# Sixteen unread TensorE products ahead of a planned attention and gate kernel

## The chip, the cores and the metric

The kernel runs on one core of a Trainium2 chip. The metric is the device time of one execution in microseconds (us). Five engines work side by side, each through its own instructions in order: TensorE (PE, with its weight loads shown apart as PEld), VectorE (DVE), ScalarE (ACT), GpSimd (POOL) and SyncE (SP, which here only issues DMAs). They wait for each other through semaphores.

## The reference: what is computed

Inputs are q, k, v of shape (4, 8, 768, 64), centroids (8, 16, 64), w_proj (512, 1536), filter_fft (768, 512) and w_out (512, 512), all float32. The output is (4, 768, 512). In the reference's terms, cut to what matters:

```
q_assign, k_assign = argmax over 16 centroids of the normed q, k
scores = q k^T / sqrt(64), -1e9 where q_assign and k_assign differ
attn = softmax(scores) @ v                      # per batch and head
x1, x2, x3 = split(attn as (4, 768, 512) @ w_proj)
x2_conv = irfft(rfft(x2) * rfft(filter_fft))    # along the 768 tokens
out = (x1 * x2_conv * x3) @ w_out
```

## The kernel before, in words

**Work.** Eight groups n of four heads (two groups for each batch) go through three steps. *Routing* turns q and k by TensorE transposes (the function `tr` in `routing`, line 592, issued at L594, for the first two groups; `tr2`, L583, later), copies them out of PSUM (helper `copy`, L265, on ACT or DVE), multiplies them with the normed centroids (`sim`, L503 for the first group, L614 later), copies that out, transposes it back (L513, L627) and lets DVE find the largest (L520 to L527, L635 to L652). The result becomes 16 more rows of the operands of the scores. *Attention* works on pairs of heads, with six steps sk of 128 keys: scores (function `sc`, issued at L73 or L75, into one PSUM bank each), exponentials on ACT (L697, L700) into a buffer p, the product with v (`pv`, L711, into the PSUM pair of banks 4 and 5), and a running sum of the p on DVE (`part` L728, `acc` L732) for the denominators. At the end of a pair ACT copies the result out (L735), the denominators go through TensorE (`den` L745) or DMAs, and DVE writes the normed result xT (L811). For the very last pair this goes without DMAs: `den` L745, `total` on ACT L751, `dT` L793, a reciprocal on DVE L796, `bc` L802, xT L811. *Hyena* takes each batch after its second group: the middle third of the projection (L845), folds on DVE (L859, L864), the spectrum (L466), its product with the filter (L875, L879), the first and last third of the projection in single products of 0.65 us (function `G`, line 904, issued at L75; its bank is emptied by a copy L913 or a multiplication L916 on DVE), the way back (function `I`, line 923, whose result DVE takes out at L941 or L951, with a copy at L939), the gate (L954) and w_out (line 964).

**Order.** None of this is issued in the order of the program text. `op` records every step with its possible engines, a guessed duration and a due time; `Plan.place` then plays the steps through in time, gives each to an engine and a PSUM bank, and among the steps that could start within 0.1 us takes the one with the earliest due time. The table NUDGE moves single due times and ONLY fixes engines, so order and banks can be set step by step. What is built is an order for each engine, which the chip then follows whatever the times are. `banks_for` gives banks by class: "head" may use banks 4 and 5 until the first `pv`, "fill" may not.

**Start.** POOL makes the identity (`constants`), the first loads of q, k and the centroids go out on SP and ACT, DVE makes the angles of the transform tables (L355 to L362) between the steps of the centroids (L319 to L330), and ACT takes their square root and the sines (L322, L365, L367), with a table load ahead of each kind. TensorE's first instructions are the six transposes of the first q (L594), then the transpose of the centroids (L333), then twelve transposes (L594), then the first eight instructions of `sim` (L503).

Of the kernel before, what the change touches and what calls it, by code (L numbers as in the profile page):

```python
# [35 lines left out]
LEAD = 2.99901  # L36
FIRST = 2
BUSY = 8.09741
# [5 lines left out]
HOLD = {"score": "score", "o": "o"}  # L44
AFTER = {"PE": .16}
OVERLAP = {"ACT": .09, "DVE": .08}
MODES = {"pv": 64, "bc": 64, "half": 64, "sim": 32, "den": 32, "score": 0, "proj": 0, "inv": 0}


def array(o, last):  # L50
# [27 lines left out]
class Plan:  # L78
# [6 lines left out]
    def op(self, eng, fn, due, r=(), w=(), alloc=None, free=(), lock=False, byts=0, after=(), kind=None, lat=0.0):  # L85
# [15 lines left out]
        for key in w:  # L101
            self.writers[key] = [o]
            self.reads[key] = []
        deps.discard(o)
        o.deps = deps
        o.left = len(deps)
        for d in deps:
            d.outs.append(o)
        for h in free:
            h.readers += 1  # L110
        self.ops.append(o)
        return o

    def place(self, free0, banks_for, switch=0.1, wait=0.1, rate=215e3, bonus=10.84378, margin=0.02195, shape=1.63806):
        free = dict(free0)
        bank_free = [0.0] * 8
        ready = {e: [] for e in free}
        pend = 0
        st = SimpleNamespace(pool=0.0, dve=0.0, bw={}, last=None, kind=None, score=0, o=0, tail=0,
                             held=dict(score=0, fill=0, o=0))  # L120
        st.scores, st.otiles = (sum(o.alloc is not None and o.alloc.cls == c for o in self.ops) for c in ("score", "o"))
        busy = dict.fromkeys(free, 0.0)

        def enqueue(o):
            o.ready = max([d.end - AFTER.get(d.on, 0.0) * (d in o.soft) + (0.06 if o.eng.keys().isdisjoint((d.on,)) or d.byts else 0.0)
                           for d in o.deps] or [0.0])
            if o.kind == "load":
                o.ready = max(o.ready, o.due - LEAD)
            for e in o.eng:
                ready[e].append(o)  # L130

        def take(o):
            if o.alloc is None:
                return
            o.alloc.ids = banks_for(o.alloc, bank_free, st, o)[0]
            for i in o.alloc.ids:
                bank_free[i] = 1e9
            st.score += o.alloc.cls == "score"
            st.o += o.alloc.cls == "o"
            st.held[HOLD.get(o.alloc.cls, "fill")] += o.alloc.n  # L140
            if o.alloc.cls != "o":
                st.tail |= st.o == st.otiles and any(i in (4, 5) for i in o.alloc.ids)

        def done(o, e, t, d, end):
            o.start, o.on = t, e
            o.end = end + AFTER.get(e, 0.0)
            if o.byts:
                s, b = max(o.end + 1.3, st.bw.get(e, 0.0)), o.byts / rate
                for f in [f for f in st.bw if f != e and st.bw[f] > s]:
                    b += min(o.byts / rate, st.bw[f] - s)  # L150
                    st.bw[f] += min(o.byts / rate, st.bw[f] - s)
                st.bw[e] = s + b
                o.end = st.bw[e] + 0.6 + o.lat
            if e == "POOL" and o.lock:
                st.pool = t + d
            if e == "DVE" and o.lock:
                st.dve = t + d
            for h in o.free:
                h.readers -= 1
                h.end = max(h.end, o.end)  # L160
                if not h.readers:
                    st.held[HOLD.get(h.cls, "fill")] -= h.n
                    for i in h.ids:
                        bank_free[i] = h.end + 0.06
            for x in o.eng:
                ready[x].remove(o)
            for x in o.outs:
                x.left -= 1
                if not x.left:
                    enqueue(x)  # L170

        for o in self.ops:
            if o.seq in ONLY:
                o.eng = {ONLY[o.seq]: o.eng[ONLY[o.seq]]}
        for o in self.ops:
            if not o.left:
                enqueue(o)
        while any(ready.values()):
            best = None
            for e, lst in ready.items():  # L180
                f = free[e]
                cand = []
                for o in lst:
                    t = max(f, o.ready)
                    m = margin if e == "PE" else 0.0
                    late = max(f, o.ready + m)
                    if o.alloc is not None:
                        ids = banks_for(o.alloc, bank_free, st, o)
                        if ids is None:
                            continue  # L190
                        t, late = max(t, ids[1]), max(late, ids[1] + m)
                    if o.lock and e in ("POOL", "DVE"):
                        t = late = max(t, st.dve if e == "POOL" else st.pool)
                    cand.append((late, o, t))
                if not cand:
                    continue
                t0 = min(c[0] for c in cand)
                c = min((c for c in cand if c[0] <= t0 + wait + 1e-9), key=lambda c: (
                    c[1].due - (bonus if e == "PE" and st.kind == "pv" == c[1].kind else 0.0)
                    + (shape if e == "PE" and array(c[1], st.last) != st.last else 0.0)  # L200
                    + (BUSY if e == "DVE" and len(c[1].eng) > 1 else 0.0)
                    + (c[0] - t0) * 20, c[1].seq))
                if best is None or (t0, c[0]) < best[0]:
                    best = ((t0, c[0]), e, c[1], c[2])
            if best is None:
                raise RuntimeError("stuck: " + repr([(e, [x.kind for x in l][:4]) for e, l in ready.items()]))
            _, e, o, t = best
            take(o)
            d = o.eng[e]
            if e == "PE":  # L210
                mode = array(o, st.last)
                if mode != st.last:
                    d += switch
                st.last, st.kind, o.whole = mode, o.kind, mode == 128
            done(o, e, t, d, t + d)
            busy[e] += d - OVERLAP.get(e, 0.0)
            free[e] = t + d - OVERLAP.get(e, 0.0)
        self.busy = busy
        self.span = max(o.end for o in self.ops)
        return sorted(self.ops, key=lambda o: (o.start, o.seq))  # L220
# [27 lines left out]
def build(T):  # L248

    P = Plan()  # L250
    op = P.op
# [31 lines left out]
    def qk(z, ch):  # L283
        return [("qkT", z, i) for i in (((0,), (1, 2)), ((0, 1), (2,)))[z % 2][ch]]

    def dma(e):
        return (T.nc.scalar if e == "ACT" else T.nc.sync).dma_start

    def alu(e):
        return T.nc.vector if e == "DVE" else T.nc.gpsimd  # L290

    EV384 = {"ACT": .465, "DVE": .55}
    EV512 = {"ACT": .585, "DVE": .68}


    qslot, loads = {}, []

    def load_qk(n, pr, j, due, after=()):
        s = qslot[n, pr, j] = len(loads) % NQK
        loads.append(1)  # L300

        return [op({"SP": .8, "ACT": .8} if n == 0 else ("SP", .8), lambda e, hp=hp: dma(e)(
            T.qkraw[s][:, :, hp], (T.q, T.k)[j][n // 2, 4 * (n % 2) + 2 * pr + hp].rearrange(
                "(p t) d -> p t d", t=NT)), due, w=[("qkraw", s, hp)], byts=196e3, kind="load", after=after, lat=.5)
            for hp in range(2)]

    def load_v(n, pr, due, after=()):
        op(("SP", .6), lambda e: T.nc.sync.dma_start(
# [73 lines left out]
    def tables(got):  # L382

        FW = [("fw", m, cs) for m in range(3) for cs in range(2)]
        fv = lambda: T.filt.rearrange("(w p m e) d -> w e p m d", w=2, p=64, m=3, e=2)
        for w_ in range(2):
            for e_ in range(2):
                op(("SP", .7), lambda e, w_=w_, e_=e_: T.nc.sync.dma_start(
                    T.f[w_][64 * e_:64 * e_ + 64], fv()[w_, e_]), 16.0, w=[("f", w_, e_)], byts=393e3, kind="load", after=got)
        for j in range(6):  # L390
            h = Bank("head")
            due = 20.0 + 2 * j

            def tr(e, j=j, h=h):
                tp = ap(h).bitcast(BF16)
                for m in range(2):
                    cols = (0, 192, 0, 192, 128, 320)[j]
# [165 lines left out]
    def routing(n):  # L563
# [41 lines left out]
        if n == 0:  # L605
            return got + first_masks(1)
        b0 = end - 24.04235
        b0 -= EARLY * (n == 1)
        h = Bank(cls, 2)

        def sim(e, h=h):
            for ch in range(2):
# [4 lines left out]
           kind="sim")  # L617
# [610 lines left out]
```

## Time and profile before

| what | value |
| --- | --- |
| median of three executions | 383.94 us (383.84 to 384.43) |
| the profiled execution | 384.85 us |
| its span, first to last instruction | 383.1 us |
| busy: PE, DVE, ACT, POOL | 364.8, 347.5, 261.6, 108.6 us |
| first PE instruction | 4.63 us |
| PE waits, longest two | 4.7 us for the first q, 2.8 us for the centroids |
| DMA | 47.19 MB, mean 123 GB/s |

All views come from one execution. The page gives busy times and 40 slices of the span. The chain of waits follows the work that ended last back from the end, each piece with its start, its length and what it was. The timeline of one engine gives start, length, line, operation, tiles and count of its instructions, merged where equal ones follow each other, and in brackets the idle time just before and what ended it. Since instructions of one engine overlap at their edges, the time from one start to the next is what one of them costs.

### The profile page before, as it was taken

The numbers are of one execution on the slowest core, as the hardware profiler recorded it, in microseconds if no ns is written. First come the engines' busy times: TensorE is split into PE (matmuls) and PEld (weight loads), VectorE is DVE, ScalarE is ACT, GpSimd is POOL, SyncE is SP. The second block draws the span as 40 slices with busy tenths as digits, with TensorE's granted clock in tenths as the row PEclk, the third lists the DMA queues.
The fourth block names the chain that finished last, engine by engine and source line by source line (L and its number), as shares of the span: only waits on it lengthen the run. The fifth ranks groups of instructions, "written<-read, shape, count | busy, mean of one in ns | idle before, by whom it ended". The sixth has DMA issues, their size and how long they took to land.

```text
span 383.1 us, 8652 instructions
## 1 busy us (share of the span) xinstructions
PE 364.8 (95%) x3323; PEld 208.3 (54%) x3328; DVE 347.5 (91%) x519; ACT 261.6 (68%) x488; POOL 108.6 (28%) x147
## 2 busy tenths in 40 slices
PE   2999998999999999999999999999999999999895
PEld 1564454445445565655555565656554565567682
DVE  8878997999899999989998999989999999899992
ACT  5996979787883978858856569688863747623332
POOL 8432101100022544123432453133320442103600
PEclk9999999999999999999999999999999999999999
DMA  9719965762578587747796876855555642110214
GB/s 221 160 47 220 164 154 135 158 146 63 128 165 157 104 130 151 126 90 122 160 144 147 165 191 134 173 72 89 103 75 132 134 105 37 46 43 2 94 74 164
DMA packets 93861, 47.19 MB, mean 123 GB/s; under 512 B 82088, under 2 KB 87676, under 8 KB 93820
## 3 DMA queue, kind: packets, MB, share of 16 engines
q1 hardware_dynamic: 88620, 37.03, 39.9%
q0 software_dynamic: 2704, 8.98, 17.6%
q10 hardware_dynamic: 2496, 0.62, 0.7%
q8 instruction: 26, 0.43, 0.5%
q14 instruction: 15, 0.12, 0.1%
HBM read 31.59 MB, written 7.40 MB: 102 GB/s over the span
## 4 chain that ended last, share of the span: by engine, by line
PE 55%; DVE 22%; DMA 9%; ACT 7%; issue 5%; SPq 1%; POOL 0%; POOLq 0%; DVEq 0%; ACTq 0%
PE bank L75 22%; PE pair L711 18%; DVE acc L732 5%; DMA rb<-dr 5%; PE bank L845 4%; ACT p L700 3%; DVE tm L875 2%; PE bank L583 2%; PE bank L594 2%; PE bank L614 1%; DVE acc L728 1%; DMA dr<-dn 1%; ACT p L697 1%; DVE xT L811 1%; PE bank L503 1%
## 5 line engine op out<-in xcount | busy, mean ns | idle before, releaser
L711 PE MATMUL pair<-p,vraw 128*64 128x385 f32 x768 | 142.5, 490 | 0.9 <-ACT osb L735 0.6
L700 ACT ACTIVATE p<-bank 128x512 f32<-128x512 f32 x192 | 108.9, 604 | 31.9 <-PE bank L75 26.5
L732 DVE TENSOR_TENSOR acc<-p,acc 128x1536 f32<-128x1536 f32 x64 | 113.0, 1765 | 4.9 <-ACT p L697 2.3
L711 PEld LDWEIGHTS pair<-p,vraw 128*64 128x64 f32 x768 | 53.7, 136 | 49.6 <-issue 42.5
L75 PE MATMUL bank<-aug,aug 80*64 80x512 bf16 (+3 forms) x688 | 75.2, 327 | 2.2 <-DVE den L753 0.5
L697 ACT ACTIVATE p<-bank 128x512 f32<-128x512 f32 x96 | 57.2, 606 | 11.6 <-PE bank L75 10.8
L75 PEld LDWEIGHTS <-aug 128*64 128x64 bf16 (+1 forms) x688 | 40.5, 109 | 38.9 <-issue 28.6
L765 POOL DMA_DIRECT2D acc<-acc x30 | 23.8, 793 | 91.1 <-DMA acc<-acc 42.6
L75 PE MATMUL bank<-xT,wpj 128*64 128x384 bf16 x488 | 44.7, 326 | 0.0
L267 POOL CAST aug<-qkP 64x768 bf16<-64x768 f32 x22 | 20.3, 927 | 71.7 <-DVE acc L732 34.1
L265 ACT COPY qkP<-bank 128x512 f32<-128x512 f32 (+1 forms) x52 | 26.7, 543 | 15.9 <-PE bank L75 8.6
L75 PEld LDWEIGHTS <-wpj 128*64 128x64 bf16 x488 | 29.6, 110 | 13.9 <-issue 3.8
L75 PEld LDWEIGHTS <-y 128*64 128x64 bf16 x512 | 25.5, 110 | 14.4 <-issue 4.4
L728 POOL TENSOR_TENSOR acc<-p,p 128x512 f32<-128x512 f32 x13 | 16.5, 1275 | 53.2 <-ACT p L700 25.7
L875 DVE TENSOR_TENSOR tm<-bank,hm 128x512 f32<-128x512 f32 x44 | 27.9, 681 | 1.0 <-POOL y L879 0.2
L728 DVE TENSOR_TENSOR acc<-p,p 128x512 f32<-128x512 f32 x35 | 24.6, 730 | 2.7 <-ACT p L697 1.7
L265 ACT CAST aug<-qkP 64x768 bf16<-64x768 f32 x29 | 24.0, 831 | 1.6 <-PE bank L75 1.1
L879 POOL TENSOR_TENSOR y<-tm 128x512 bf16<-128x512 f32 x17 | 21.7, 1289 | 10.5 <-DVE tm L875 6.3
L845 PE MATMUL bank<-wpj,xT 128*64 128x512 bf16 x192 | 22.7, 380 | 0.9 <-DVE xT L811 0.9
L75 PE MATMUL bank<-wout,y 128*64 128x512 bf16 x192 | 22.9, 379 | 0.0
L735 ACT COPY osb<-pair 128x770 f32<-128x770 f32 x16 | 12.9, 808 | 9.6 <-PE pair L711 9.5
L811 DVE SCALAR_TENSOR_TENSOR xT<-osb,rb 128x768 bf16<-128x768 f32 x15 | 15.2, 1012 | 3.9 <-DMA rb<-dr 3.9
(161 smaller groups left out, 440.7 us busy)
## 6 DMA issues: line engine op xcount, KB each, us to landing
qkraw<-in_k_dram SPq DMA_DIRECT2D x32, 192.0 KB, 4.6
vraw<-in_v_dram SPq DMA_DIRECT2D x16, 384.0 KB, 4.3
rb<-dr SPq DMA_DIRECT2D x30, 192.0 KB, 3.3
out_dram<-ob SPq DMA_DIRECT2D x11, 512.0 KB, 2.8
qkraw<-in_q_dram SPq DMA_DIRECT2D x29, 192.0 KB, 3.9
acc<-acc POOLq DMA_DIRECT2D x10, 384.0 KB, 4.9
acc<-acc POOLq DMA_DIRECT2D x10, 192.0 KB, 4.1
y<-in_moe_filter_fft_dram SPq DMA_DIRECT2D x4, 384.0 KB, 8.9
```

The lines of the kernel that those rows point to most:

```text
L75: T.nc.tensor.matmul(out[64 * i:64 * i + 64], lhsT[:, 64 * i:64 * i + 64], rhs, start=start, stop=stop)
L265: T.nc.scalar.copy(out, in_)
L267: (T.nc.vector if e == "DVE" else T.nc.gpsimd).tensor_copy(out, in_)
L697: T.nc.scalar.activation(o, ap(h).rearrange("p (a b) -> p a b", a=2), Act.Exp, scale=0.125)
L700: T.nc.scalar.activation(flat(s)[:, lo:lo + 512], ap(h), Act.Exp, scale=0.125)
L711: T.nc.tensor.matmul(o[64 * hp:64 * hp + 64, ch, :385], T.vraw[vs][:, hp, sk * D:(sk + 1) * D], T.p[slots[sk]][:, hp, 384 * ch:384 * ch + ...
L728: alu(e).tensor_tensor(o, x, y, op=Alu.add)
L732: T.nc.vector.tensor_tensor(T.acc[os], T.p[slots[sk]][:, :, :S], T.acc[os], op=Alu.add)
L765: op(("POOL", .8), lambda e, rows=rows: T.nc.gpsimd.dma_start(flat_()[:rows], flat_()[rows:2 * rows], accum_op=Alu.add), te, r=[], w=AK, b ...
L845: T.nc.tensor.matmul(ap(h)[64 * i:64 * i + 64], T.xT[xs][:, kt, c:c + 64], T.wpj[:, kt, DM:2 * DM], start=kt == 0, stop=kt == ND - 1)
L875: op(("DVE", .68), lambda e, i=i, cs=cs, r=r, h=h: T.nc.vector.tensor_tensor(T.tm[r][:, cs], ap(h), hmrow(i, (0, 2, 2, 3)[2 * r + cs]), op ...
L879: op({"POOL": 1.5, "DVE": .68}, lambda e, i=i, r=r: alu(e).tensor_tensor(T.y[:, i, r], T.tm[r][:, 0], T.tm[r][:, 1], op=Alu.add if r else ...
```

## The change

A new function `warm` adds one DVE step, which writes ones into 640 columns of the tile mt (bfloat16), and sixteen TensorE products that read only this tile: eight of 128x128 by 128x512 and, behind the first transposes of q, eight of 128x128 by 128x256. Each writes a PSUM bank that nothing reads before a later product overwrites it. They are recorded just before the tables. The constants of the planner change too (LEAD, BUSY, bonus and shape become 0, a weight in the choice falls from 20 to 0.2), a rule about DVE and POOL, some bank classes, and NUDGE and ONLY are new tables that set the order again.

```diff
-LEAD = 2.99901
+LEAD = 0.0
...
-BUSY = 8.09741
+BUSY = 0.0
...
-    def place(self, free0, banks_for, switch=0.1, wait=0.1, rate=215e3, bonus=10.84378, margin=0.02195, shape=1.63806):
+    def place(self, free0, banks_for, switch=0.1, wait=0.1, rate=215e3, bonus=0.0, margin=0.02195, shape=0.0):
...
-                        t = late = max(t, st.dve if e == "POOL" else st.pool)
+                        t = max(t, st.dve + 0.06 if e == "POOL" else st.pool)
+                        late = max(late, t)
...
-                    + (c[0] - t0) * 20, c[1].seq))
+                    + (c[0] - t0) * 0.2, c[1].seq))
...
+    def warm():
+        op(("DVE", .25), lambda e: T.nc.vector.memset(T.mt[:, :640], 1.0), -1, w=["mt"])
+        for i in range(8 + 8):
+            h = Bank("head")
+            n = 512 if i < 8 else 256
+            op(("PE", .02), lambda e, h=h, n=n: T.nc.tensor.matmul(
+                ap(h)[:, :n], T.mt[:, 512:640], T.mt[:, :n], start=True, stop=True), .1 + .02 * i, r=["mt"], w=[h], alloc=h,
+               free=[h], kind="warm", after=turns[:1] if i >= 8 else ())
...
+    warm()
     tables(got)
```

Here `turns` lists the first transposes of q and k. Laid side by side, the orders of the two built programs differ beyond the seventeen new instructions in these places (times are those of the trace of before):

- Near 22 us ACT copies one turned k out seven places earlier. Near 75 us SP issues one rb load ahead of the transposing DMA L657, near 95 us DVE does one `part` before xT, near 150 us PE does one score before two G.
- From 226 to 247 us DVE takes one L916 two steps earlier and another eight, and the steps L775 to L778 of one denominator come later, SP's loads with them.
- From 253 to 276 us PE does five G and one I before the second score of the next pair, and a sixth G before its ninth. Three of these G had come after that pair's fifth `pv`.
- From 319 to 327 us PE does one `den` four products later and the I behind it earlier; DVE does an L916 and a copy of I (L267 for L939) before an `acc`.
- From 332 to 348 us DVE does the second L916 and an `acc` before the xT at 333.09, and three steps (two L941, one L916) before the last pair's xT instead of behind it; PE does two G before the last `den` and before `dT` which had stood behind `bc`.
- 120 of the 531 PSUM allocations follow another step in their bank than before.

## The prediction

> **What bounds the kernel now.** I read the page's totals first, then the chain of waits, then the timelines of single engines where the diff acts.
>
> ```profile
> span 383.1 us, 8652 instructions
> PE 364.8 (95%) x3323; PEld 208.3 (54%) x3328; DVE 347.5 (91%) x519; ACT 261.6 (68%) x488; POOL 108.6 (28%) x147
> ```
>
> PE is busy in all but 18 us of the span: 4.7 and 2.8 at the start, some 5 at the end, about 5.5 in between. So the time is PE's work plus its few waits, and a mere exchange of PE work costs nothing unless it makes a wait. The places to look at are the start, where the products are added, and the end, where 353 to 362 us of the chain lie mostly on DVE.
>
> At the start the chain of waits shows one operation with two durations (start, length, what):
>
> ```profile
> 9.35 2.56 PE bank L594 x12
> 11.91 2.71 PE bank L503 x8
> 14.62 0.81 PE bank L594 x6
> 16.32 1.63 PE bank L503 x8
> ```
>
> Twelve transposes take 2.56 us, 0.21 each; six later ones 0.81. The weight loads of those six start every 0.107 us (six in 0.64). Eight instructions of `sim` take 2.71 us and later 1.63. PE works at half rate until about 14.5 us and then at full rate, with no change of shape. The page's PEclk row reads 9 in every slice, so it does not show this; only durations do.
>
> [...]
>
> **The change part by part.** Sums are against the profiled execution, 384.85 us: 383.1 of span and 1.75 around it. It lies 0.91 above the median of 383.94; I carry differences over to that median.
>
> *The writing of ones.* DVE's first instruction now waits until 1.35 us for the identity, and the other engines' first ones after the common start stand at 0.74. So 0.6 us are free. The write's own duration is not in the trace: 0.19 (the copy L450) to 0.78 (L355, which runs beside POOL). I take 0.4, nearest to the cast L1027 of 0.40: hidden, cost 0. At 0.78 it costs 0.2, since DVE has no gap up to the centroids' sum that ACT's root waits for.
>
> *The sixteen products.* Two half-width scores of 512 columns run side by side in 0.22 us at full rate (the chain's L75 at 328.59), so a product of 512 columns is an estimated 0.43 us at half rate: eight fill 1.2 to 4.65 us, and the transposes start at 4.67 when q lands. Cover: PE's 4.7 us idle; without it, up to 1.5 us more are covered, because ACT takes these transposes out only at 7.80. The second eight cost 0.9 to 1.7 us and fit the 2.75 us before L333 at 8.94. Their banks are written again only by PE, in order. Cost 0.
>
> *What they bring.* If PE is at full rate from 8.94 on, 12 transposes and 8 `sim` instructions lose some 1.3 and 1.1 us. But ACT has its own queue:
>
> ```profile
> 12.36 0.63 ACT L367 ACTIVATE fw<-ob,half_pi 128x384 bf16<-128x384 f32 x1
> 13.41 0.47 ACT L265 COPY sim<-bank 64x384 f32<-64x384 f32 x1 [0.43 <-PE bank L503]
> 13.79 0.52 ACT L365 ACTIVATE fw<-tm 128x384 bf16<-128x384 f32 x1
> 14.69 0.47 ACT L265 COPY sim<-bank 64x384 f32<-64x384 f32 x1 [0.38 <-PE bank L503]
> 15.18 1.28 ACT L379 ACT_TABLE_LOAD   x1
> ```
>
> From 6.08 to 19.9 us ACT waits for PE only in the two brackets, 0.43 and 0.38. The `sim` cannot start before ACT has copied the second pair out (10.75 to 11.59), so at full rate its halves end near 11.9 and 12.5, both ahead of ACT. **0.8 us** go; what is late next is ACT itself, without gap to 19.9. DVE's largest (L520) comes 1.2 earlier, but the second `simT` waits for ACT's copies at 17.94, so 0.8 is what reaches the `rows` transposes (L537, 19.65) and the first scores. Loads start earlier by as much. The ACT copy moved near 22 us delays two exponentials by 0.47; `pv` at 24.79 waits for DVE's L558 (ends 24.64) anyway. 0.
>
> *The middle.* 75, 95 and 150 us: PE has no wait there that these decide; DVE even idles 1.64 us at 95, where the moved step fits. 0. From 226 to 247 us one L916 comes early to DVE and may wait 0.5 for its G, while another frees its bank four us sooner, and PE waits only 0.2: 0, bounds -0.4 and +0.5. Then:
>
> ```profile
> 257.12 2.12 PE L75 MATMUL bank<-xT,wpj 128*64 128x384 bf16 x24
> ...
> 260.60 1.47 PE L711 MATMUL pair<-p,vraw 128*64 128x385 f32 x8
> ...
> 273.29 1.98 PE L75 MATMUL bank<-xT,wpj 128*64 128x384 bf16 x22
> ```
>
> The three G at 273.29 (1.95) move ahead of `pv` at 260.60, to 262.55. But the pair's second score now stands behind five G and an I and ends near 260.4 instead of 256.5. ACT's order has the exponential that `pv` needs fifth from there, at 0.49 apart: it ends near 263.05. PE waits **0.5 us**, and later scores keep up. Bounds 0 and 0.6; I take 0.5, the worked value, since PE is in the chain without gap to 283.5.
>
> *The end.* DVE in its timeline:
>
> ```profile
> 331.18 0.22 DVE L778 RECIPROCAL dn<-dn 128x12 f32<-128x12 f32 x1
> 332.61 0.56 DVE L916 TENSOR_TENSOR x<-bank,x 128x384 f32<-128x384 f32 x1 [1.22 <-PE bank L75]
> 333.09 1.01 DVE L811 SCALAR_TENSOR_TENSOR xT<-osb,rb 128x768 bf16<-128x768 f32 x1
> 334.01 0.55 DVE L916 TENSOR_TENSOR x<-bank,x 128x384 f32<-128x384 f32 x1
> ...
> 343.74 1.13 DVE L811 SCALAR_TENSOR_TENSOR xT<-osb,bank 128x384 bf16<-128x384 f32 x2
> 344.79 1.01 DVE L941 TENSOR_TENSOR sd<-bank,od 128x384 f32<-128x384 f32 x2
> ```
>
> From 332.6 to 354 us DVE has no gap, and it sets the end through L864, L875 and POOL's L879. In the new order it idles 1.5 us near 320 to 322.5 (L941 waits for an ACT copy that stands behind an exponential, a copy waits for its I), which the 1.22 at 332.61 nearly swallows. Then the second L916 stands directly behind the first and waits for the last of four G (PE ends them at 333.7): with both, the last `acc` ends near 338.7 instead of 338.02, **0.7 us**. Behind it two L941 and an L916 (0.93 + 0.47) move ahead of the last xT, which ends near 346.95 instead of 344.87. The moved steps are no loss themselves, but PE's last projection parts (L848) and DVE's copy of them, 345.72 now, must follow the xT, and DVE idles the 0.4 us from xT to the copy, which L941 had filled. **0.4 us**. PE's own wait of 1.3 there is covered by the 1.04 it waits at 362.65. End: 1.1; bounds 0.3 (if only the bare hand-over shows) and 1.6.
>
> Sum: -0.8 + 0.5 + 1.1 = **+0.8 us**: 385.65 for a profiled execution, **384.7** for the median.
>
> **The rivals.**
>
> *The moves cost nothing.* DVE's waits fall in gaps that exist (1.22 before L916, PE's 1.04 at the end), and only the start counts: 383.94 - 0.8 = 383.1, not slower. For it: 5.5 us of scattered waits can soak up shifts. Against: DVE's row at 343.74 has no gap behind it.
>
> *The start gives nothing.* If PE reached full rate at 12.4 instead of 14.5 us in the runs that were timed, the first half of `sim` ended near 12.6, ACT would take it at 12.99, and both brackets were empty already. Then 383.94 + 0.5 + 1.1 = 385.5. The point that decides is 12.6 us. For it: the three times spread by 0.6. Against: no trace shows it. [...]
>
> *The products don't raise the rate*, because PE falls back over the 1 to 2 us before 8.94: also 385.5. After the 1.04 us wait at 362.65 PE's products run as fast as before, which speaks against it.
>
> **How the numbers follow.** Forecast 384.7 (384.2 to 385.1): 0.42. Moves free, 383.1 (up to 383.6): 0.24. Start gives nothing, 385.5 (up to 386): 0.22; products without effect, the same time: 0.05. The rest, 0.07, in between or worse. What a measurement can tell from no change is about 0.2%, 0.77 us: faster is below 383.17, slower above 384.71. Faster 0.2 (most of the second case), slower 0.44 (half of the forecast, and the two at 385.5), same 0.36. The range 383.1 to 385.7 leaves out some 0.2.
>
> **What would show it.** In the new profile: twelve L594 in about 1.5 us near 9, L503 in 1.3 to 1.6; no bracket on ACT's two `sim` copies and the table load near 14.4; the first `pv` near 24.0. Then PE idle before the first `pv` of the pair near 262, an L916 on DVE waiting near 333, xT of the last pair ending 2 us later than in before against the same `pv`, and the last products starting 0.8 later. I am wrong if the twelve still take 2.5 us, or if the shift of 0.8 gained at 24 us is still there at 362.

## The result, and the profile after

The kernel after takes 386.89 us (median of five, 386.45 to 388.38), the kernel before 384.08 beside it: a ratio of 1.0083, 95% interval 1.0059 to 1.0107. It is 2.8 us slower; 0.8 was forecast, and 385.7 was the end of the range. Its profiled execution took 388.38, span 386.2: 3.1 more of span than the first profile of before, and 0.4 more around it.

The page of after: PE is busy 4.7 us longer than before. The products take 5.1 us, while the transposes and `sim` behind them get 2.3 shorter, so some 1.9 lie elsewhere. DVE is busy as long as before.

```profile
span 386.2 us, 8694 instructions
PE 369.5 (96%) x3350; PEld 210.2 (54%) x3350; DVE 347.6 (90%) x520; ACT 261.7 (68%) x488; POOL 108.6 (28%) x147
```

**The start** did what the products are for. PE's timeline, first two lines of before, then after:

```profile
9.15 2.77 PE L594 MATMUL bank<-ident,qkraw 128*128 128x128 f32 x12
11.84 2.77 PE L503 MATMUL bank<-qkP,cbd 128*32 128x384 f32 x8
```

```profile
1.59 3.60 PE L1052 MATMUL bank<-mt 128*128 128x512 bf16 x8 [1.59 <-DVE mt L1048]
4.98 1.49 PE L596 MATMUL bank<-ident,qkraw 128*128 128x128 f32 x6
6.26 1.47 PE L1052 MATMUL bank<-mt 128*128 128x256 bf16 x8
8.93 0.30 PE L335 MATMUL bank<-ident,sd 128*64 128x128 f32 x1 [1.20 <-DVE sd L332]
9.07 1.48 PE L596 MATMUL bank<-ident,qkraw 128*128 128x128 f32 x12
10.96 1.77 PE L505 MATMUL bank<-qkP,cbd 128*32 128x384 f32 x8 [0.41 <-ACT fw L367]
```

The twelve transposes take 1.48 us instead of 2.77, the first `sim` 1.77 instead of 2.77. On ACT both brackets before the copies of `sim` are gone:

```profile
12.87 0.47 ACT L266 COPY sim<-bank 64x384 f32<-64x384 f32 x1
13.23 0.53 ACT L367 ACTIVATE fw<-tm 128x384 bf16<-128x384 f32 x1
13.65 0.47 ACT L266 COPY sim<-bank 64x384 f32<-64x384 f32 x1
14.14 1.28 ACT L381 ACT_TABLE_LOAD   x1
...
21.00 0.58 ACT L703 ACTIVATE p<-bank 128x512 f32<-128x512 f32 x1
21.49 0.82 ACT L266 COPY qkP<-bank 128x384 f32<-128x384 f32 x2
22.22 0.58 ACT L700 ACTIVATE p<-bank 128x512 f32<-128x512 f32 x1
```

In before the exponentials stood so:

```profile
22.05 0.58 ACT L700 ACTIVATE p<-bank 128x512 f32<-128x512 f32 x1
...
22.89 0.58 ACT L697 ACTIVATE p<-bank 128x512 f32<-128x512 f32 x1
```

The table load starts 1.04 earlier, the first exponential too (22.05 to 21.00). The next one already stands only 0.67 earlier: the copy moved there costs 0.37, and the first `pv` starts at 24.10 instead of 24.79.

**The middle.** DVE, then PE, of after; behind them two lines of before for the last readings:

```profile
227.25 0.56 DVE L919 TENSOR_TENSOR x<-bank,x 128x384 f32<-128x384 f32 x1 [0.46 <-PE bank L75]
...
239.80 0.56 DVE L919 TENSOR_TENSOR x<-bank,x 128x384 f32<-128x384 f32 x1 [0.57 <-ACT x L266]
...
248.10 1.75 DVE L735 TENSOR_TENSOR acc<-p,acc 128x1536 f32<-128x1536 f32 x1
250.05 1.02 DVE L814 SCALAR_TENSOR_TENSOR xT<-osb,rb 128x768 bf16<-128x768 f32 x1 [0.20 <-DMA rb<-dr]
...
257.31 0.55 DVE L919 TENSOR_TENSOR x<-bank,x 128x384 f32<-128x384 f32 x1
```

```profile
257.92 0.85 PE L75 MATMUL bank<-inv,y 128*64 128x192 bf16 x16 [0.34 <-DVE x L919]
...
292.14 0.81 PE L848 MATMUL bank<-wpj,xT 128*64 128x512 bf16 x6
294.24 4.72 PE L848 MATMUL bank<-wpj,xT 128*64 128x512 bf16 x42 [1.28 <-DVE xT L814]
```

```profile
256.31 0.56 DVE L916 TENSOR_TENSOR x<-bank,x 128x384 f32<-128x384 f32 x1
...
292.47 4.72 PE L845 MATMUL bank<-wpj,xT 128*64 128x512 bf16 x42 [0.49 <-DVE xT L811]
```

Two multiplications that were moved forward wait, 0.46 for a G and 0.57 for a copy on ACT, and the one that PE waits for at 257.92 (it starts at 257.31) stands 1.00 later than in before (256.31). The last wait, 1.28 for an xT that waits for rb, was 0.49 in before.

**The end.** DVE of after, whose row had no gap from 332.6 to 354 in before:

```profile
323.00 1.02 DVE L944 TENSOR_TENSOR sd<-bank,od 128x384 f32<-128x384 f32 x2 [1.14 <-ACT od L266]
...
335.70 0.56 DVE L919 TENSOR_TENSOR x<-bank,x 128x384 f32<-128x384 f32 x1 [0.63 <-PE bank L75]
336.18 1.75 DVE L735 TENSOR_TENSOR acc<-p,acc 128x1536 f32<-128x1536 f32 x1
...
347.69 1.13 DVE L814 SCALAR_TENSOR_TENSOR xT<-osb,bank 128x384 bf16<-128x384 f32 x2
349.32 0.69 DVE L268 COPY tm<-bank 128x512 f32<-128x512 f32 x1 [0.50 <-PE bank L848]
```

All three waits that the prediction placed here are there, at 323, 335.7 and 349.3. The same steps of before stand at 321.22, 334.01 and 345.72, without a wait.

### The profile page after: what moved, and what is told of

Its sections match the earlier page's. It is cut to its first block, busy times and chain, and to the rows that moved or that the text cites. A ratio compares the mean times of both kernels' runs of the same rounds, so it can differ in the third digit from the quotient of the medians.

```text
span 386.2 us, 8694 instructions
## 1 busy us (share of the span) xinstructions
PE 369.5 (96%) x3350; PEld 210.2 (54%) x3350; DVE 347.6 (90%) x520; ACT 261.7 (68%) x488; POOL 108.6 (28%) x147
## 4 chain that ended last, share of the span: by engine, by line
PE 45%; DVE 25%; ACT 12%; DMA 9%; issue 6%; SPq 1%; POOL 0%; POOLq 0%; ACTq 0%; DVEq 0%
PE bank L75 20%; PE pair L714 14%; DVE acc L735 8%; DMA rb<-dr 6%; PE bank L848 3%; ACT p L703 3%; ACT aug L266 3%; DVE tm L878 2%; DMA dr<-dn 2%; PE bank L585 2%; DVE tm L862 1%; ACT p L700 1%; DVE xT L814 1%; DVE uv L867 1%; DVE acc L731 1%
## 5 line engine op out<-in xcount | busy, mean ns | idle before, releaser
L75 PE MATMUL bank<-aug,aug 128*64 128x512 bf16 (+3 forms) x692 | 76.2, 327 | 2.5 <-DVE x L268 0.6
L75 PEld LDWEIGHTS <-aug 80*64 80x64 bf16 (+1 forms) x692 | 41.9, 109 | 39.9 <-issue 29.6
L75 PE MATMUL bank<-xT,wpj 128*64 128x384 bf16 x496 | 45.9, 326 | 0.0
L75 PEld LDWEIGHTS <-wpj 128*64 128x64 bf16 x496 | 30.6, 110 | 12.7 <-issue 3.3
L848 PE MATMUL bank<-wpj,xT 128*64 128x512 bf16 x192 | 23.1, 380 | 2.6 <-DVE xT L814 2.5
```

What stands on the lines that cost most here:

```text
L75: T.nc.tensor.matmul(out[64 * i:64 * i + 64], lhsT[:, 64 * i:64 * i + 64], rhs, start=start, stop=stop)
L848: T.nc.tensor.matmul(ap(h)[64 * i:64 * i + 64], T.xT[xs][:, kt, c:c + 64], T.wpj[:, kt, DM:2 * DM], start=kt == 0, stop=kt == ND - 1)
```

## Where the time went: one measure for all profiles

The exponentials come in the same sequence in nearly all kernels. So the start of each, less the start of the same one in the first profile of before, is a running balance, and its steps show where time is lost or won. The table gives the steps of it in us (minus is earlier; the last column is read from DVE's L859 to L875 and the span). "p." marks kernels with the products.

| profile | first exp. | 23-150 | 150-214 | 214-286 | 286-298 | 298-end |
| --- | --- | --- | --- | --- | --- | --- |
| after, p. | -1.04 | +0.32 | +0.34 | +1.14 | +1.01 | +1.37 |
| after again, p. | -1.06 | +0.34 | -0.47 | +1.15 | +0.71 | +1.39 |
| order alone | -0.01 | +0.35 | -0.58 | +1.22 | -0.68 | +1.72 |
| before again | -0.13 | -0.02 | -0.69 | 0 | -0.67 | 0 |
| products alone, p. | -1.06 | -0.02 | -0.15 | +0.06 | +0.42 | 0 |
| end, own banks | -0.30 | -0.01 | -1.33 | +0.01 | -0.27 | +1.94 |
| middle, own banks | -0.24 | -0.03 | -0.37 | +1.40 | -0.65 | 0 |
| turns 247-285 | -0.82 | -0.01 | -0.08 | +0.71 | -0.51 | 0 |
| turns 219-245 | -0.74 | +0.01 | -1.26 | +0.88 | +0.01 | 0 |
| the same without SP's | -1.04 | -0.03 | -0.58 | +0.87 | -0.04 | +0.16 |
| SP's turns 219-245 | -0.01 | -0.02 | -0.77 | +1.62 | -0.11 | 0 |
| rb first | -1.00 | -0.02 | -0.33 | -0.01 | -0.68 | 0 |
| rb first, p. | -1.05 | -0.02 | +0.14 | +0.08 | -0.67 | 0 |
| rb at three places | -0.62 | -0.03 | -0.89 | +1.25 | -0.68 | 0 |
| the same, p. | -1.04 | -0.02 | -0.43 | +2.36 | -0.67 | 0 |
| rb at three places, same banks | -0.41 | -0.02 | -0.53 | 0 | -0.67 | 0 |
| the same, p. | -1.06 | -0.01 | -1.07 | +0.07 | -0.63 | 0 |

In the three profiles with the whole order of after, three columns repeat: 0.32 to 0.35 near 23 us, 1.14 to 1.22 from 214 to 286, 1.37 to 1.72 at the end. Their sum, 2.8 to 3.3, is about the 2.9 that the order costs by the times. The other three differ between executions of the same kernel: the two profiles of before are 0.69 and 0.67 apart in two of them.

## The experiments

**Products alone, and order alone.** In the first the order and banks of before are kept, and the products are issued by hand:

```diff
+    def ones(n):
+        for i in range(8):
+            nc.tensor.matmul(T.bank[6 + i % 2][:, :n], T.mt[:, 512:640], T.mt[:, :n], start=True, stop=True)
+    nc.vector.memset(T.mt[:, :640], 1.0)
+    ones(512)
     for o in order:
+        seen += o.on == "PE"
+        if o.on == "PE" and seen == 3:
+            ones(256)
```

> The kernel before with only the writing of ones and the sixteen products added by hand; every other step keeps its place and its bank. Theory (the products gain at the start, the changed order loses it later): the 1.04 us that the profile after shows at the table load near 14 us last to the end, 383.0 to 383.4 against 384.08. Rival 1 (what is gained at the start meets transfers that come no earlier, so it is lost again at the next wait for one): 383.9 to 384.2, with the bracket before a later xT or first scores longer by the gain. Rival 2 (the products themselves cost later, through the earlier loads): above 385.

384.06 us against 383.96, ratio 1.0002 (0.9986 to 1.0017): no change, by the time. In its profile the first exponential is 1.06 earlier, 1.17 are there at 286 us, and 0.42 is given back before the projection at 291.72, which waits 0.89 for xT instead of 0.49. So rival 1 is what the time shows. The profile's span is 0.75 below that of before's first profile, but this one lies 1.1 above the mean span of before's 17 executions beside it (382.0).

The second is after with `lambda e: None` in place of the writing and of each product:

> The kernel after with neither the products nor the writing of ones, all else in the order and the banks of after. Theory (order): some 0.7 to 1.0 above the kernel after, 387.6 to 387.9. Rival 2 (the products cost later): 384 to 385. If the products gain nothing in timed runs: 386.9.

386.83, ratio 1.0086 (1.0068 to 1.0104). All of the loss is the order's. The products, on top of it, change nothing in the time (386.89 and 387.16 with them), as the last sentence of the expectation had it; the 387.6 to 387.9 of the theory is missed.

**Parts of the order, first try.** Here the steps of a stretch change places among themselves as in after; where a bank was then still held, the step took the first free one.

> The kernel before with the products, and with all changes of order of after on PE, DVE, ACT and POOL, but with the order of before on SP (the load of v behind the two loads of rb near 241 us, dr ahead of dd near 225). Theory S (a good part of the middle's loss comes through SP: rb is issued 1.6 us later behind the load of v, and xT, which starts 2.9 us later, pushes DVE's copies by 1.0): 385.6 to 386.1. Rival P (PE's order of G ahead of the scores sets all of it): 386.7 to 387.0, as after.

398.72, ratio 1.0401 (1.0376 to 1.0427).

> The kernel before without products, with the changes of order from 312 us of the plan on alone (PE, DVE, ACT, POOL). The prediction's term for the end is +1.1, so 385.2. The profile after has a shift of 1.76 us at 319 us and 3.1 at the end, so +1.4 by that: 385.5. Rival (the end's new order costs nothing by itself, and the shift there follows from what comes late into it): 384.1.

391.93, ratio 1.0232 (1.0195 to 1.0269). Both are far slower than after with all of its order, so they miss every expectation and can't decide between them, but they tell something of banks. The end's turns, PE:

```profile
330.55 0.41 PE L75 MATMUL bank<-aug,aug 80*64 80x512 bf16 x2 [2.07 <-DVE sd L941]
...
343.39 0.84 PE L75 MATMUL bank<-xT,wpj 128*64 128x384 bf16 x8 [2.23 <-DVE x L916]
```

Two waits of over 2 us, for banks that DVE had yet to empty; four steps had been given the first free bank. From here on the planner itself placed the new order, each engine bound to its queue, and chose the banks by its times:

```diff
-                for o in lst:
+                for o in lst if not QUEUE else [x for x in lst if x.seq == QUEUE[e][heads[e]]]:
...
+def turned(T):
+    for o in build(T)[1]:
+        QUEUE.setdefault(o.on, []).append(o.seq)
+    for e, lists in TURNS.items():
+        for new in lists:
+            for i, s in zip(sorted(QUEUE[e].index(s) for s in new), new):
+                QUEUE[e][i] = s
+    return build(T)[1]
```

**The two kernels again, the end and the middle.**

> The kernel before once more, for a second profile. The products alone brought the first exponential 1.06 us earlier, and yet 384.06 against 383.96. Theory R (the landing of rb near 291 us, on which xT and the projection L845 wait, differs from execution to execution by about 1 us, so that the first profile of before is one draw): every step up to 286 us within 0.3 of the first profile, the wait before L845 near 292 anywhere from 0 to 1.3 instead of 0.49. Rival (a fixed kernel, fixed waits): all waits within 0.1 of the first profile, and a span of 382 to 383 by other means.

A single execution, 383.33 us. The wait before L845 near 292 is gone, so it does differ between executions, as theory R has it; span 381.6, and all exponentials to 150 us within 0.15. The expected 0.3 up to 286 us was too narrow: 0.69 more was won from 150 to 214.

> The kernel after once more, on the chip of the next two. Median 386.5 to 387.0. Theory R: the wait before the projection near 294 us is anywhere from 0 to 1.3 in the second profile, and the steps up to 283 us are within 0.2 of the first. The order's own loss, from 245 to 283 us, is 1.3 again.

387.16, ratio 1.0078 (1.0050 to 1.0106), just above the expected 387.0. The wait before the projection is 1.00 and the middle's loss 1.15, but up to 283 us the two profiles of after are 0.8 apart, where 0.2 was expected.

> As the kernel of the end's turns alone (no products; the changes of order from 312 us of the plan on), but with the banks that the planner gives to that order, not banks given by hand. By the profile after (shift of 1.8 at 319 us, 3.1 at the end) 385.3 to 385.5; by the prediction's term 385.1. Rival (the end's order costs nothing, its waits follow from what comes late into it): 384.0.

386.10, ratio 1.0053 (1.0036 to 1.0070): 1.8 to 2.0 us. More than expected. The rival falls: the end costs by itself, 1.94 of span in the profile against 1.4 inside after (34 steps come behind another step in their bank than in before), and 0.36 more around the span (2.15 against 1.79, means of 12 and 23 runs).

> No products; the changes of order from 219 to 285 us of the plan alone, on all engines, SP's included, with the banks that the planner gives. By the profile after, the shift between 245 and 283 us is 1.3, so 385.3. The prediction's term is 0.5, so 384.5. Rival (most of the loss is the end's): 384.1.

385.10, ratio 1.0028 (1.0012 to 1.0045): 1.1 us by the means, 1.40 by the profile. The prediction's 0.5 lies at the lower end of the interval and below every profile of this order, so it is most likely too small.

**The middle, in parts.** These four are single executions, of 384.47, 383.74, 385.69 and 384.31 us. Such times tell nothing at this size, so what follows is read from inside their profiles, by the table's column from 214 to 286.

> No products; of the changes of order only those on PE, ACT and DVE from 247 to 285 us of the plan, where five G and an I go ahead of the pair's second score. The prediction's term for it: +0.5 between 245 and 283 us, with PE waiting ahead of the first product of the pair near 262. Theory S (the late rb of 241 us, and the steps before 247, carry the rest of the 1.2 to 1.4 that the whole middle shows): 0.5 to 0.7. Rival P (PE's order carries it all): 1.2 to 1.4.

+0.71, and no wait over 0.08 in PE's timeline there, so the forecast wait does not come. The loss shows only when equal work is compared: from the `pv` at 251.60 to the `pv` at 275.00, 23.40 us, where before has 252.52 to 275.26, 22.74. Of these 0.66, 0.53 lie in the 64 scores (5.88 us against 5.35, from start to start).

```profile
257.72 1.47 PE L75 MATMUL bank<-xT,wpj 128*64 128x384 bf16 x16
259.02 1.71 PE L75 MATMUL bank<-aug,aug 80*64 80x256 bf16 x20
260.81 0.84 PE L75 MATMUL bank<-xT,wpj 128*64 128x384 bf16 x8
261.45 0.74 PE L75 MATMUL bank<-aug,aug 128*64 128x512 bf16 x4
262.00 1.46 PE L711 MATMUL pair<-p,vraw 128*64 128x385 f32 x7
```

The pair's scores stand behind five G and an I, as forecast; what this costs is spread over the scores, not in one bracket before `pv`. Why they take longer is not shown. The planner also gave other banks: 27 steps come behind another step in their bank than in before, and the 0.71 includes what that costs.

> No products; of the changes of order only those from 219 to 245 us of the plan, with SP's: dr behind dd, the load of v ahead of rb. Theory S: xT near 247 starts 2.5 to 3 us later, DVE's copies behind it some 1 us, and PE shows 0.4 to 0.7 of new wait before the inverse products near 258. The prediction took 0 for this stretch, bounds -0.4 and +0.5. Rival P: 0 by 283 us, since PE in the old order does not wait for those copies.

+0.88, with xT 2.9 later against the exponentials. Near theory S's numbers, so far.

> No products; only SP's changes of order from 219 to 245 us: dd and dp ahead of dr and rb near 227, the load of v ahead of rb near 241. Theory S: xT near 247 is later by 1 us or more, and 0.5 to 0.9 is lost between 214 and 283 us. Rival (DVE's order, where the sum that dr comes from stands behind five other steps): xT later by less than 0.7, and 0 to 0.2 lost.

+1.62, with 16 steps behind another step in their bank. By itself SP's order does cost: DVE waits for rb before xT, and PE then for the L916 behind it.

```profile
248.19 1.02 DVE L811 SCALAR_TENSOR_TENSOR xT<-osb,rb 128x768 bf16<-128x768 f32 x1 [0.97 <-DMA rb<-dr]
...
257.92 2.14 PE L75 MATMUL bank<-xT,wpj 128*64 128x384 bf16 x24 [0.72 <-DVE x L916]
```

> No products; only the changes of order on PE, DVE, ACT and POOL from 219 to 245 us. Theory S: dr about 1.8 us later near 241, by DVE's order, but rb with it alone, and at most 0.3 lost by 283 us. Rival: 0.6 to 0.9 lost by 283 us.

+0.87, and xT again 2.9 later, with the same banks as the run before last and only SP's order put back. So once DVE has its new order, in which an `acc` stands ahead of this xT, SP's order adds nothing, and theory S falls for the kernel after. The mechanism is DVE's queue. DVE of this kernel, then PE:

```profile
225.97 0.56 DVE L916 TENSOR_TENSOR x<-bank,x 128x384 f32<-128x384 f32 x1 [0.46 <-PE bank L75]
...
238.53 0.56 DVE L916 TENSOR_TENSOR x<-bank,x 128x384 f32<-128x384 f32 x1 [0.56 <-ACT x L265]
...
255.72 0.55 DVE L916 TENSOR_TENSOR x<-bank,x 128x384 f32<-128x384 f32 x1
257.20 0.56 DVE L267 COPY x<-bank 128x384 f32<-128x384 f32 x1 [0.93 <-PE bank L75]
```

```profile
254.11 1.26 PE L75 MATMUL bank<-aug,aug 80*64 80x256 bf16 x14
256.33 2.14 PE L75 MATMUL bank<-xT,wpj 128*64 128x384 bf16 x24 [0.95 <-DVE x L916]
```

Both L916 that were moved forward on DVE wait, one 0.46 for its G and the other 0.56 for ACT's copy. DVE has no other gap from 226 us on, so it carries these 1.02 for up to 30 us, to the L916 at 255.72 (1.06 late against the exponentials), which empties the bank that PE needs at 256.33. In before DVE has no wait from 225 to 257 us, and PE none there. Here too 20 steps come behind another step in their bank than in before, but the last of them stands near 250 us, and the exponentials have lost nothing by 255. The loss falls at this one wait.

**The wait for rb.** Does the late rb near 291 us take what the start gains? On SP the two loads of rb go ahead of the load of v, `TURNS = {"SP": [[1417, 1416, 1698]]}`; all banks stay.

> The kernel before without products; on SP alone the two loads of rb near 285 us go ahead of the load of v that stood before them (order ohT, rb, rb, v). Theory R (the landing of rb near 291 us sets the wait before the projection L845 near 292): rb lands 1 us or more earlier after its dr, no wait there, and 0 to 0.5 off the median of before (waits of 0.49 and 0 in its two profiles), 383.8 to 384.2. Rival (the load of v is no part of rb's time): rb still takes 8.1 to 8.8 us from the issue of dr to xT.

383.19, ratio 0.9978 (0.9965 to 0.9992): faster than before, by more than theory R's number (383.8 to 384.2), and no wait before L845:

```profile
289.80 5.35 PE L845 MATMUL bank<-wpj,xT 128*64 128x512 bf16 x48
```

> The same with the writing of ones and the sixteen products. Theory R (the 1 us gained at the start is given back at the wait for rb near 292, because rb lands no earlier there): the wait is gone here, so the gain reaches the end: 0.8 to 1.1 below the kernel without products, 382.8 to 383.2. Rival (the gain is lost elsewhere, in the waits near 206 or in none that a profile shows): within 0.3 of the kernel without products.

383.21, ratio 0.9980 (0.9966 to 0.9993). The wait is gone here too, and yet 0.02 from its pair: theory R's number missed, the rival's met. Near 206 us this profile waits 0.60 for xT, its pair 0.67.

> No products; on SP the loads of rb go ahead of the load of v near 160 and near 285 us, and ahead of the third load of aug near 200. Theory R (xT waits for rb near 166, 206 and 292 us, and PE behind it): the waits there shrink by 0.5 to 1, and the time falls below that of the kernel with the one place changed (383.19): 382.5 to 383.0. Rival (the waits near 166 and 206 are set by how long rb takes and not by its place): 383.1 to 383.3.

384.22, ratio 1.0014 (0.9998 to 1.0030): slower than both expectations.

> The same with the products. In the eight kernels without them the rate doubled between 11.9 and 14.6 us, so that the first exponential stood 0 to 1.0 ahead of the first profile, 0.36 on the mean; with them always 1.06: 0.7 to gain on the mean. Theory R: with the waits for rb gone 0.4 to 0.7 of it reaches the end, 0.4 to 0.7 below the kernel without products. Rival (it is lost in something else): within 0.2 of it, as in the two pairs before.

384.77, ratio 1.0030 (1.0012 to 1.0048): 0.55 slower than the kernel without the products, at the same banks, where both expectations had it faster or even. The wait near 206 fell to 0.12 and 0.18 in the two, but the planner had given both other banks than before's (18 steps behind another one), and 1.25 and 2.36 were lost from 214 to 286. So the same with the banks of before:

> No products; rb ahead of the load of v near 160 and 285 us and ahead of the third load of aug near 200, with every bank and every other engine's order as before. Theory R: the wait before L845 near 206 falls to 0.2 or less, none near 170 and 292, nothing lost from 245 to 283, and 382.6 to 383.0. Rival (the waits only move to the next transfer): 383.2 to 383.8.

383.12, ratio 0.9988 (0.9974 to 1.0002). The wait near 206 is 0.60 here, not 0.2, and the time lies between the two expectations.

> The same with the products. Theory R: 0.3 to 0.6 below the kernel without them (0.7 gained at the start on the mean of the profiles, 0.1 more time around the span). Rival (what the start gains is lost in transfers whose time does not follow PE): within 0.2 of it.

382.54, ratio 0.9968 (0.9943 to 0.9993): 0.58 below its pair by the medians, 0.32 by the means (382.72 and 383.04, each of 12 runs that spread by 2 to 3 us). It is the fastest kernel of all, but its interval overlaps its pair's. Of the five pairs that differ in the products alone, the medians differ by +0.10 (products alone), +0.06 (after against order alone), +0.02, +0.55 and -0.58: on the whole the products brought nothing.

## Why the prediction was wrong, step by step

*The direction* was right, and the order's part was the cause, as argued. The size was not. The prediction added -0.8 for the start, 0 for the copy on ACT, 0.5 for the middle and 1.1 for the end. The runs show about 0, 0.35, 1.15 and 1.4. Without the start the prediction had 1.6 for the order, and order alone measures 2.9. Two steps failed: that the start's gain reaches the end, and that the stretch of 226 to 247 us costs nothing.

*The writing of ones and the products*: right. The writing took 0.59 us (0.4 was taken, 0.78 the bound). Eight products of 512 columns took 3.60 us (0.43 each was the estimate), the second eight 1.47 (0.9 to 1.7), and PE starts L335 at 8.93, against 8.94. Only `sim` is a little longer than forecast, 1.77 for 1.3 to 1.6.

*"0.8 us go", the start*: **this step failed as a difference of times.** That the products would have PE at full rate by 8.94 was the author's estimate, which no profile of before shows; in after the twelve transposes behind them take 1.48 us instead of 2.77. In the profile the step held, 1.04 and, with the moved copy, 0.67. But the first profile of before was at the slow end of a range. In 13 profiles of kernels without the products the twelve L594 always take 2.73 to 2.77, but the `sim` behind them 1.48 to 2.78, because the rate doubles (one transpose every 0.213 us near 9, every 0.107 near 14.6 in the first profile) anywhere from 11.8 us to about 14.6:

```profile
9.14 2.77 PE L594 MATMUL bank<-ident,qkraw 128*128 128x128 f32 x12
11.84 2.65 PE L503 MATMUL bank<-qkP,cbd 128*32 128x384 f32 x8
```

```profile
9.14 2.73 PE L594 MATMUL bank<-ident,qkraw 128*128 128x128 f32 x12
11.80 1.48 PE L503 MATMUL bank<-qkP,cbd 128*32 128x384 f32 x8
```

The first is the second profile of before, the other the turns of 219 to 245 without SP's, both with before's start. The first exponential stands 0 to 1.04 ahead of the first profile, 0.41 on the mean; with the products always 1.04 to 1.07. So 0.65 was to be had on the mean. This is the second rival's condition (rate doubled by 12.6), met in two of the 13 (`sim` in 1.48 and 1.63 us) and in part in most others. With the same work ahead of it, the place of the doubling varied by some 2.8 us over the 13 profiles; what sets it is not shown.

*What is left of it does not reach the end either; why is open.* A part goes at the wait for rb. Before the projection near 292, ten profiles without the products and with the old place of rb wait 0 to 0.50 (0.25 on the mean), four with them 0.89 to 1.28. Putting rb ahead of the load of v takes the wait away in all six kernels that do it. So in these four profiles the wait takes 0.6 to 1.0 back. It isn't shown to be the whole cause: with the wait gone, the gain still misses the time in one pair (0.02) and shows as 0.58 in another, within the scatter. Nor is it shown why xT waits longer with the products. From rb's second issue to xT it is 6.1 to 6.7 us in three profiles with them, but 5.5 in the fourth, and 4.9 to 5.9 without. An early start alone does not do it: the turns of 219 to 245 without SP's are as early at the first exponential (1.04) without products, and wait 0.45. Another 0.1 of the gain goes in the time around the span: 1.90 to 1.93 on the mean of the four kernels that got the products by hand on before's order on PE, 1.78 to 1.80 in the same without them.

*"The ACT copy moved near 22 us ... 0"*: 0.32 to 0.37. DVE's L558, which was to hide the delay, comes late itself: with the products alone it starts at 22.90, in after at 23.23, behind a wait of 0.84 for PE.

*"The middle", 0.5*: 1.15 in place. The term for PE's order was close in size (0.71 alone), but not in kind: the wait before `pv` did not come, and the scores took longer instead. **The stretch of 226 to 247, set to 0, is the step of it that failed.** The wait of 0.5 of one L916 was seen and written off because PE waited little there; the other, which was to free its bank sooner, waits as long (0.56). Together they cost 0.87: DVE has no gap in which to lose them before PE needs a bank from it, 30 and 18 us later. The two parts don't add up: 0.71 and 0.87 alone, 1.14 to 1.40 together.

*"The end", 1.1*: 1.37 to 1.39, right in kind and place. The last `acc` ends at 340.52, which is 338.02 and the 1.76 of delay on entry and 0.74 (0.7 was forecast), and the copy of L848's parts waits 0.50 (0.4). Some 0.4 more stands in the time around the span (2.17 on the mean of after's runs, 1.79 of before's), which no profile shows. The end's turns alone have 0.36 of it, but order alone, with the same turns, only 0.16 (1.95), so where it comes from is open.

*The rivals.* "The moves cost nothing" falls with order alone. "The start gives nothing" was right of the time, but in its reason only in part (an early doubling explains 0.41 of the 1.06), and wrong in its sum, since it took the same 1.6 for the order. "The products don't raise the rate" falls with 1.48 for 2.77.

## What to carry to other kernels

A wait on an engine that is nearly full is not free because the bound engine does not wait there: follow the delay along that engine's queue to the next bank or buffer that it hands over, and charge it there (here 0.46 and 0.56 on DVE, and 0.95 on PE 30 and 18 us later). Before pricing a gain from one profile, ask whether the thing gained varies by itself; more profiles of the kernel before would have shown 0.4 of the 1.06 us to be chance. And a changed order is not separable from its banks: the end's turns cost 8.0 us with first free banks and 1.8 with those of the planner.

## What the runs showed of the hardware

The doubling of PE's rate, with the same instructions before it, fell anywhere within some 2.8 us (from 11.8 to about 14.6, 13 profiles). With sixteen unread products ahead, and a gap of 1.20 us behind them, it lay ahead of 9.07 us in after: the twelve transposes from there take 1.48 us, against 2.73 to 2.77 in the 13. In all seven profiles with the products the first exponential stands 1.04 to 1.07 ahead of that of the first profile of before. With two transfers of rb (192 KB each) behind the same load of v, 4.9 to 6.7 us passed from the second issue to the step that reads them, a range of 1.8 us beside a gain of 1 at the start.
